# Plain fp32 operands on TensorE for the first batch element of a local attention, with its probabilities transposed there

## The chip, the cores and the metric

The kernel runs on one core of a Trainium2 chip. The metric is the device time of one execution in microseconds, the median of the runs; three runs of the kernel before took 1001.03 to 1006.15 us, with a median of 1003.59.

## What is computed

```python
def _attn_ref(q, k, v, n_global, n_local):          # 4 elements, 8 heads, 768 positions, 64 wide
    scores = scale * np.matmul(q, k.transpose(0, 1, 3, 2))
    keep = is_global | is_local                     # first 8 keys, or the last 96 up to the query
    scores = np.where(keep, scores + bias, -1e9)    # bias: -slope of the head * distance
    a = np.exp(scores - max); a = a / (sum + 1e-9)
    return np.matmul(a, v)
...
x = attn_out as 3072 tokens x 512
h = max(x @ w1, x @ w2, x @ w3, 0); x = h @ w_out   # "MoE 1", no experts, 768 wide
e_idx = argmax(x @ w_gate)                          # "MoE 2": each token goes to one of 8 experts
out[token] = gate * eom * (max(x @ w1[e], 0) @ w2[e])
```

q, k, v are float32; w1, w2, w3 and w_out arrive as float64.

## The kernel before

Attention goes by 24 query tiles of 128 positions, six to a batch element (`QT`), each with 8 heads. A tile sees at most 232 keys: 8 global ones, the 96 before it and its own 128 (the first tile of an element only its own 128).

All products keep fp32's precision by split operands. `a_T` transposes q and k on TensorE, ScalarE writes the high part as fp32r and VectorE the rest (`qh`, `ql`); `a_scores` then does three matmuls per head, high x high, high x low, low x high, in two halves of four heads, after which VectorE adds the bias and takes the minimum (L826) and ScalarE the exponential (L833). `a_trans` splits the probabilities of a half into two fp16 parts (`nat`, L847 and the subtraction at L189) and has the DMA queue transpose them (L853). `a_v` scales v by a power of two and splits it into two fp16 parts; `a_vg` brings the rows of the global keys along and rescales them. `a_out` multiplies with three fp16 matmuls per head and key block (L883), divides on VectorE (L889) and stores the tile; the x of the tiles goes to MoE 1.

MoE 1 takes tiles in passes: eight of two tiles (`m_1`, L976: 216 fp32r matmuls of 256 columns for w1, w2 and w3, 72 each), then two of four tiles with 512 columns. Pass 0 goes through all of w1, then w2, then w3. x is transposed and split first (`split_T`, L917). `m_2` multiplies with w_out (L1036), and `m_route` sends the tokens to their experts. The float64 rows of the weights, 12 for w1 to w3 and 6 for w_out, are loaded as raw words and turned into two fp32r parts by `convert`: ScalarE (L603), VectorE (L605 and twice L608), ScalarE again (L613) and POOL (L189). `pad_rows` stores rows of padding when attention is over. After phase 1 comes a loop over pairs of expert tiles with rows of 25 us per step, bound by TensorE.

The order of all this is written out by `Plan.run`: a list scheduler in the kernel's own Python that takes, again and again, the operation which can start first by its table of costs, ties going to the lower rank. Each engine, and SyncE with the DMA queue, then runs its list strictly in order. A change to one step's costs or waits thus moves others too.

Of the kernel before, what the change touches and what calls it, by code (L numbers as in the profile page):

```python
# [266 lines left out]
def local_attention_moe_kernel(  # L267
# [25 lines left out]
    QT = S // P  # L293
    NTILE = NT // P

    NPAIR = NTILE // 2 - 4
# [187 lines left out]
    for tag, n in (("qk", 4),):  # L484
        stock(tag, [at.tile([P, H, HD], F32, name=f"{tag}n{c}") for c in range(n)])
    stock("va", [at.tile([P, 2, D], F16, name=f"va{c}") for c in range(4)])
    vs = at.tile([P, NTILE, 4], F32, name="vs")
    stock("qT", [[at.tile([P, H // 2, P], F32R, name=n) for n in ("qh", "ql")]])
    stock("kT", [at.tile([P, 2, H // 2, NW], F32R, name=f"k{c}") for c in range(2)])
    stock("sp", [at.tile([P, 4, NW], F32, name=f"sp{c}") for c in range(2)])  # L490


    nat_t = [at.tile([P, 2, 4, 2 * P], F16, name=f"nat{c}") for c in range(2)]
    stock("nat", nat_t)
    stock("aT", [at.tile([P, 2, 4, 2, P], F16, name=f"aT{c}") for c in range(2)])
    stock("xo", [at.tile([P, D], F32, name="xo")])
# [4 lines left out]

    scales = [-(2.0 ** (8.0 * j / H)) / HD**0.5 for j in range(2)]

    def tables(rel, key, mask, tmp):
# [132 lines left out]
    def done(tag, u):  # L637

        n = uses[tag, u] = uses.get((tag, u), 0) + 1
        last = u % QT == QT - 1  # L640

        if n == (3 - last if tag == "k" else 1 + (u % QT < QT - 1) + (u % QT < QT - 2)):
            give(dict(k="kT").get(tag, tag), A[tag, u])

    left0 = [0]

    def first_done():
        left0[0] += 1
        if left0[0] == 3:
# [5 lines left out]
    def a_load(u, name):  # L655
        b, i = divmod(u, QT)
        if u == 0:
            t = Buf(first["qkv".index(name)])
            t.written = t.last = 5.5 + 1.46 * "qkv".index(name)
        else:  # L660
            t = yield take("qk")
        if u or name == "v":
            yield dma(P * D * 4, w=[t], rate=DMA_RATE_ROWS)
            src = [x[b, :, i * P : (i + 1) * P, :].rearrange("h t d -> t h d") for x in (dict(q=q, k=k, v=v)[name], vd)]
            if name == "v":
                nc.sync.dma_start(out=t.t, in_=src[1], cond=dense > 0, cond_hint=False)
                yield op(DMA, 0.5)
                nc.sync.dma_start(out=t.t, in_=src[0], cond=dense < 1, cond_hint=True)
            else:
                nc.sync.dma_start(out=t.t, in_=src[0])  # L670
        return t

    def a_v(u):

        if u:
            yield need(("va", u - 1))
        t = yield from a_load(u, "v")
        va = yield take("va")
        vf = t.t.rearrange("p h d -> p (h d)")
        b, i = divmod(u, QT)  # L680
        sb = VS[u]
        total, top, scale, ratio = [vs[:, u, n : n + 1] for n in range(4)]
        before = vs[:, u - 1, 1:2] if i else VLOW
# [24 lines left out]
        if u:  # L708
            give("qk", t)
        else:  # L710
            first_done()
        A["va", u] = va
        state("va", u)

    def a_vg(u):

        yield need(("va", u), ("o", u - 1))
        va = A["va", u - 1]
        rows = slice(G0, P - NPREV)
        first_ = u % QT == 1  # L720
        src = va if first_ else A["va", u - 2]
        yield dma(0, [src], [va])
        nc.sync.dma_start(out=va.t[rows], in_=src.t[:NG] if first_ else src.t[rows])
        if not first_:
            done("va", u - 2)
        eng = yield op((ACT, POOL), {ACT: act(2 * D), POOL: pool(2 * D)}, [VS[u], va], [va])
        if eng == ACT:
            nc.scalar.mul(out=va.t, in_=va.t, mul=vs[:, u, 3:4])
        else:
            nc.gpsimd.tensor_scalar(out=va.t, in0=va.t, scalar1=vs[:, u, 3:4], scalar2=None, op0=ALU.mult)  # L730
        state("vg", u)

    def a_T(u, name):
# [9 lines left out]
        else:  # L743
            new = yield take("qT")
        A[name, u] = new
        bank = yield take("bank")
# [4 lines left out]
        if u:  # L751
            give("qk", t)
        else:
            first_done()
        if name == "q":
            h, l = new.t[0], new.t[1]
# [13 lines left out]
        if name == "k" and i:  # L770
            old = A["k", u - 1]
            g0 = NB if i == 1 else 0
            yield op(ACT, act(H * NG), [old], [new])
            nc.scalar.copy(out=new.t[:, :, :, :NG], in_=old.t[:, :, :, g0 : g0 + NG].bitcast(F32))
# [5 lines left out]
    def a_scores(u, qd):  # L780
# [25 lines left out]
        for hp in range(2):  # L806
            for j in range(2):
                h = 2 * (2 * qd + hp) + j
                o = sp.t[:, 2 * hp + j, n0:]
                x = sc[j][:, hp, :nw_]  # L810
# [26 lines left out]
    def a_trans(u, qd):  # L837
        i = u % QT
        n0 = NB if i == 0 else 0
        yield need(("s", u, qd), *([("t", u, 0)] if qd else [("t", u - 1, 1)] if u else []))  # L840
        sp = A["sp", u, qd]
        nat = yield take("nat")
        h, l = [nat.t[:, n, :, G0 + n0 :] for n in range(2)]
        x = sp.t[:, :, n0:]
        n = 4 * (NW - n0)
# [4 lines left out]
        give("sp", sp)  # L850
        aT = yield take("aT")
        yield dma(P * 16 * P * 2, [nat], [aT], True, DMA_RATE_ROWS)
        nc.sync.dma_start_transpose(  # L853
# [6 lines left out]
    def a_out(u):  # L860
# [3 lines left out]
        sm = ms.t[1]  # L864
        va, vb = A["va", u], A["va", u - 1] if i else None
        yield op(DVE, 0.37, [ms, VS[u]], [ms])
        nc.vector.tensor_scalar(out=sm, in0=sm, scalar1=1.0e-9, scalar2=vs[:, u, 2:3], op0=ALU.add, op1=ALU.mult)
        nc.vector.reciprocal(out=sm, in_=sm)
        bank = yield take("bank")
        po = bank.t.rearrange("p (h d) -> p h d", d=HD)  # L870
        for h in range(H):
# [3 lines left out]
            for part, vp in ((1, va), (0, vb)):  # L875
                if vp is None:
                    continue
                for n, m_ in ((0, 2), (1, 1)):
# [24 lines left out]
        if vb:  # L903
            done("va", u - 1)

# [761 lines left out]
    with tc.manual_schedule(engines={ET.PE, ET.Activation, ET.DVE, ET.Pool, ET.SP}):  # L1667
# [83 lines left out]
```

## Time and profile before

| | |
|---|---|
| Median of three runs | 1003.59 us |
| The profiled execution | 1000.66 us, of which its span 998.8 |
| TensorE matmuls busy | 929.9 us (93%) |
| TensorE weight loads busy | 798.7 us (80%) |
| VectorE busy | 650.0 us (65%) |
| ScalarE busy | 518.7 us (52%) |
| GpSimd (POOL) busy | 184.9 us (19%) |
| Mean granted TensorE clock | 0.983 |

Busy time of matmuls includes their way through the array, so neighbours overlap: rates are read from the starts of instructions that follow each other. PE is TensorE's matmuls, PEld its weight loads, DVE VectorE, ACT ScalarE, SP the engine that issues the DMAs. A name in brackets behind a row is what ended the idle time before it.

### The profile page before, as it was taken

How to read it: one execution, taken by the hardware profiler on the slowest of the kernel's cores; microseconds unless marked ns; L12 is line 12 of the kernel's file. 1: busy time of each engine (PE TensorE's matmuls, PEld its weight loads, DVE VectorE, ACT ScalarE, POOL GpSimd, SP SyncE). 2: the span in 40 equal slices, each digit the busy share in tenths (PEclk: the TensorE clock that was granted, in tenths of full speed). 3: DMA queues.
4: the chain of work that ended last, by engine and by line, in shares of the span. 5: the costliest groups of instructions: out<-in, count | busy, mean ns of one | idle time of the engine just before them, and what ended most of it. 6: DMA issues, size and time to landing. Idle time of an engine off the chain costs nothing. (4 is left out here: it accounts for less than half of the span.)

```text
span 998.8 us, 19937 instructions
## 1 busy us (share of the span) xinstructions
PE 929.9 (93%) x6640; PEld 798.7 (80%) x6640; DVE 650.0 (65%) x1761; ACT 518.7 (52%) x1111; POOL 184.9 (19%) x242
## 2 busy tenths in 40 slices
PE   2486899999999999999799999999999999999996
PEld 2385788989999999999588787778888888888884
DVE  5989877777777777764433435676666666666664
ACT  4767567666556675752212312435555555555552
POOL 2544324322221321120000101120000000000000
PEclk9997999999999999999799999999999999999998
DMA  7889288667757585643711106166666666666665
GB/s 202 231 218 231 65 148 162 148 137 162 149 121 154 124 175 123 150 97 95 203 43 43 43 22 230 44 232 230 209 201 210 205 210 201 213 210 197 210 219 176
DMA packets 222798, 160.80 MB, mean 161 GB/s; under 512 B 181344, under 2 KB 181344, under 8 KB 222724
## 3 DMA queue, kind: packets, MB, share of 16 engines
q1 hardware_dynamic: 218562, 147.23, 55.5%
q0 software_dynamic: 4160, 12.62, 3.5%
q8 instruction: 41, 0.67, 0.3%
q14 instruction: 33, 0.27, 0.1%
q10 hardware_dynamic: 2, 0.00, 0.0%
HBM read 118.56 MB, written 23.11 MB: 142 GB/s over the span
## 5 line engine op out<-in xcount | busy, mean ns | idle before, releaser
L976 PE MATMUL bank<-xT,w 128*128 128x256 f32 x1728 | 233.5, 290 | 2.0 <-DVE xT L189 1.0
L976 PEld LDWEIGHTS bank<-xT,w 128*128 128x128 f32 x1728 | 217.3, 194 | 7.7 <-ACT xT L920 3.4
L833 ACT ACTIVATE sp<-sp,mn 128x232 f32<-128x232 f32 (+1 forms) x192 | 90.3, 471 | 44.9 <-DVE mn L826 42.9
L976 PE MATMUL bank<-wq,w 128*128 128x512 f32 x432 | 102.9, 397 | 3.3 <-DVE hm L998 2.4
L1458 PE MATMUL bank<-w,hh 128*128 128x512 f32 x426 | 103.3, 394 | 0.0
L976 PEld LDWEIGHTS bank<-wq,w 128*128 128x128 f32 x432 | 81.7, 191 | 21.9 <-DVE hm L998 3.7
L1458 PEld LDWEIGHTS bank<-w,hh 128*128 128x128 f32 x426 | 78.9, 188 | 16.4
L998 DVE TENSOR_TENSOR hm<-hm,bank 128x512 f32<-128x512 f32 x72 | 49.2, 685 | 59.8 <-PE bank L976 58.9
L1537 ACT ACTIVATE hm<-bank 128x512 f32<-128x512 f32 x52 | 31.0, 597 | 93.0 <-PE bank L1531 86.9
L1531 PE MATMUL bank<-wq,xT 128*128 128x512 f32 x312 | 76.5, 394 | 1.2 <-ACTq L1708 1.2
L1036 PE MATMUL bank<-w,hh 128*128 128x512 f32 x288 | 75.8, 404 | 0.0
L1531 PEld LDWEIGHTS bank<-wq,xT 128*128 128x128 f32 x312 | 57.5, 188 | 12.8 <-issue 1.6
L826 DVE CUSTOM_DVE_ANT_0 sp<-bank,bias 128x232 f32<-128x232 f32 x160 | 60.0, 389 | 10.5 <-PE bank L802 10.1
L703 POOL TENSOR_SCALAR qkn<-qkn,vs 128x512 f32<-128x512 f32 x23 | 38.3, 1667 | 142.8 <-DVE vs L698 53.7
L802 PE MATMUL bank<-k,qh 64*128 64x232 f32 (+1 forms) x384 | 43.9, 318 | 20.8 <-ACT k L776 16.4
L1136 POOL DMA_INDIRECT xs<-x2r,di x24 | 24.5, 1022 | 205.9 <-DVE cco L1439 61.9
L189 DVE TENSOR_TENSOR wq<-ws_more,wq 128x1024 fp32r<-128x1024 f32 x42 | 51.3, 1222 | 15.4 <-ACT wq L1382 15.0
L1036 PEld LDWEIGHTS bank<-w,hh 128*128 128x128 f32 x288 | 51.1, 189 | 9.1
L802 PEld LDWEIGHTS bank<-k,qh 64*128 64x128 f32 x384 | 32.2, 205 | 29.9 <-ACT k L776 17.5
L189 DVE TENSOR_TENSOR w<-ws_more,w 128x1024 fp32r<-128x1024 f32 x42 | 51.4, 1225 | 5.8 <-ACT w L1382 5.8
L189 DVE TENSOR_TENSOR nat<-sp,nat 128x928 f16<-128x928 f32 (+1 forms) x46 | 53.3, 1160 | 0.6
L189 POOL TENSOR_TENSOR seen<-x,dco 128x1 f32<-128x1 f32 x14 | 3.4, 245 | 271.2 <-DVE x L1463 271.2
(265 smaller groups left out, 1780.4 us busy)
## 6 DMA issues: line engine op xcount, KB each, us to landing
ws_more<-in_moe_w_dram SPq DMA_DIRECT2D x90, 512.0 KB, 4.4
bias<-in_moe_w_dram SPq DMA_DIRECT2D x19, 512.0 KB, 3.5
ws<-in_moe_w_dram SPq DMA_DIRECT2D x19, 512.0 KB, 4.7
raw<-in_moe_w_dram SPq DMA_DIRECT2D x12, 768.0 KB
x2r<-xs SPq DMA_DIRECT2D x30, 257.0 KB, 3.7
qkn<-in_q_dram SPq DMA_DIRECT2D x23, 256.0 KB
qkn<-in_k_dram SPq DMA_DIRECT2D x23, 256.0 KB
qkn<-vd SPq DMA_DIRECT2D x23, 256.0 KB
```

Source lines behind the costliest of these rows:

```text
L189: eng.tensor_tensor(out=out, in0=in0, in1=in1, op=ALU.subtract)
L703: nc.gpsimd.tensor_scalar(out=vf, in0=vf, scalar1=scale, scalar2=None, op0=ALU.mult)
L802: nc.tensor.matmul(sc[j][:, hp, :nw_], lhsT=x, rhs=y, start=(n < 2), stop=(n >= len(terms) - 2))
L826: nc.vector.tensor_tensor_reduce(out=o[:, g:], in0=x[:, g:], in1=bias[:, pr, n0 + g :], scale=scale, scalar=low, op0=ALU.add, op1=ALU.min, ...
L833: nc.scalar.activation(out=o, in_=o, func=AF.Exp, scale=-1.0, bias=mn[:, h : h + 1], accum_out=sm[:, h : h + 1])
L976: nc.tensor.matmul(pj[:, f2, :], lhsT=w_at(j, part, d)[:, fs], rhs=X[:, d, :], start=(d + n == 0), stop=(d == KD - 1 and n == 2))
L998: nc.vector.tensor_max(out=hv, in0=hv, in1=pj)
L1036: nc.tensor.matmul(bank.t, lhsT=X[:, f, t * P : (t + 1) * P], rhs=w_at(3, part, f), start=(f + n == 0), stop=(f == KF - 1 and n == 2))
L1136: i = nc.gpsimd.indirect_dma_start(out=xs[:, :], out_offset=bass.IndirectOffsetOnAxis(ap=di[:, 0:1], axis=0), in_=x2.t[:, :], in_offset=None)
L1458: nc.tensor.matmul(py, lhsT=at(A_), rhs=w, start=(f + m == 0), stop=(last and m == 2))
L1531: nc.tensor.matmul(ph, lhsT=xT[A_][:, d, :], rhs=W[d][B_][:, b], start=(d + m == 0), stop=(d == KD - 1 and m == 2))
L1537: nc.scalar.activation(out=hm_t[f], in_=ph, func=AF.Relu)
```

## The change

The six tiles of the first batch element (`u < EARLY`) keep q, k and v as plain fp32. Scores are one matmul per head instead of three, the output one per head and key block instead of three. The probabilities stay fp32 and are transposed by TensorE into a PSUM bank, 128 keys at a time, which ScalarE or VectorE copies out. v is loaded straight into its place, with no scaling or parts. The buffers get their old shapes and types back (`renewed`) when the tiles of the second element first take them; the `nat` buffers are cleared by POOL after the first output (`clear_nat`), and `sp` has 24 columns of zeros in front. The rest of the kernel is as it was, but for the order.

```diff
+    EARLY = 6
...
+    def clear_nat():
+        yield need(("o", 0))
+        for t in nat_t:
+            yield op(POOL, 1.2)
+            nc.gpsimd.memset(t[:, :, :, :P], 0.0)
+        state("nat")
...
 def a_v(u, again=False):
+        if u < EARLY and not again:
+            va = yield take("va")
+            yield from a_load(u, "v", va)
+            A["va", u] = va
+            state("va", u)
+            return
...
 def a_T(u, name):
+        if u < EARLY:
+            eng = yield op((ACT, DVE), {ACT: act(D), DVE: dve(D)}, [bank], [new], port=False)
+            if name == "q" and eng == ACT:
+                nc.scalar.mul(out=new.t[0], in_=pt, mul=qs)
...
+            if name == "k" and i:
+                old = A["k", u - 1]
+                g0 = NB if i == 1 else 0
+                for n0, n1, o0 in ((0, NG, g0), (NG, NB, NW - NPREV)):
+                    n = (n1 - n0) * H // 2
+                    eng = yield op((ACT, DVE, POOL), {ACT: act(n), DVE: dve(n // 2), POOL: pool(n)}, [old], [new])
...
 def a_scores(u, qd):
-            terms = [(r, j, q_.t[x][r, pr], k_.t[r, y, pr, n0:]) for x, y in TERMS for j, r in enumerate(rows)]
-            yield op(PE, 0.1 + len(terms) // 2 * 0.109, [q_, k_], [b0, b1])
+            terms = [(r, j, q_.t[x][r, pr], k_.t[r, y, pr, n0:]) for x, y in (TERMS if u >= EARLY else TERMS[:1]) for j, r in enumerate(rows)]
+            yield op(PE, 0.1 + (len(terms) // 2 * 0.109 if u >= EARLY else 4 * 0.109), [q_, k_], [b0, b1])
...
 def a_trans(u, qd):
+        if u < EARLY:
+            aT = yield take("aT")
+            for part in range(i == 0, 2):
+                bank = yield take("bank")
+                pt = bank.t.rearrange("p (a b) -> p a b", b=P)
+                for h in range(4):
+                    yield op(PE, 0.109, [sp], [bank])
+                    nc.tensor.transpose(pt[:, h, :], sp.t[:, h, part * P : (part + 1) * P], ident)
+                eng = yield op((ACT, DVE), {ACT: act(D), DVE: dve(D)}, [bank], [aT], port=False)
+                (nc.scalar.copy if eng == ACT else nc.vector.tensor_copy)(out=aT.t[:, part], in_=pt)
+                give("bank", bank)
+            give("sp", sp)
...
 def a_out(u):
+                if u < EARLY:
+                    terms.append((aT.t[:, part, h % 4, :], vp.t[:, c]))
+                    continue
...
-            yield op(PE, len(terms) * 0.029, [aT, va] + ([vb] if vb else []), [bank])
+            yield op(PE, len(terms) * (0.029 if u >= EARLY else 0.13), [aT, va] + ([vb] if vb else []), [bank])
...
+        if u == EARLY - 1 and EARLY % QT:
+            plan.add(a_v(u, True), (2, u, 1), HOLD_A)
...
-        for t in nat_t:
-            nc.vector.memset(t[:, :, :, :P], 0.0)
+        for t in sp_t:
+            nc.vector.memset(t[:, :, :G0], 0.0)
+        plan.add(clear_nat(), (5, 0))
```

Three places show how the order moves. The first is SyncE's queue in the start (before; `first` and `qkn` hold q, k and v, `raw` the words of weight rows, `aT` the transposed probabilities):

```order
L668 DMA first_87<-in_v_dram 128x8x64
L670 DMA qkn_561<-in_q_dram 128x8x64
L670 DMA qkn_562<-in_k_dram 128x8x64
L589 DMA raw_75<-in_moe_w_dram 128x1536 x2
L853 DMA_TRANSPOSE aT_578<-nat_576 128x16x128
L853 DMA_TRANSPOSE aT_579<-nat_577 128x16x128
```

The same queue with the change (`vf` is the fp32 v):

```order
L712 DMA vf_565<-in_v_dram 128x8x64
L712 DMA vf_566<-in_v_dram 128x8x64
L714 DMA qkn_561<-in_q_dram 128x8x64
L714 DMA qkn_562<-in_k_dram 128x8x64
L712 DMA vf_567<-in_v_dram 128x8x64
L624 DMA raw_75<-in_moe_w_dram 128x1536
L712 DMA vf_568<-in_v_dram 128x8x64
```

The transposes are gone from the queue, and the v loads of tiles 1 to 3 stand ahead of weight rows.

The second is VectorE's queue up to the first tile's output, before (L826 and L819 are the bias and minimum, printed as ISA):

```order
L608 SCALAR_TENSOR_TENSOR x2r<-raw_74,x2r 128x768
L847 CAST nat_577<-sp_575 128x4x128
L189 TENSOR_TENSOR nat_577<-sp_575,nat_577 128x4x128
L189 TENSOR_TENSOR k_573<-bank_520,k_573 128x4x128
L867 TENSOR_SCALAR sm_582<-sm_582,vs 128x8
L868 RECIPROCAL sm_582<-sm_582 128x8
L608 SCALAR_TENSOR_TENSOR x2r<-raw_74,x2r 128x768
```

and with the change:

```order
L643 SCALAR_TENSOR_TENSOR x2r<-raw_74,x2r 128x768
L836 COPY kf_572<-kf_571 128x4x96
L948 COPY aTf_578<-bank_517 128x512
L982 TENSOR_SCALAR sm_581<-sm_581 128x8
L985 RECIPROCAL sm_581<-sm_581 128x8
```

The two fp16 steps and k's low part are gone; a copy of k and one eviction of transposed probabilities stand in their place.

The third is TensorE's queue from the last attention output on, before (`x` is a tile of MoE 1's input, `wq` holds the transposed x of the passes of four tiles):

```order
L883 MATMUL bank_522<-va_568,aT_579 128x64
...
L917 MATMUL bank_523<-ident,x_536 128x128 x4
L917 MATMUL bank_518<-ident,x_537 128x128 x4
...
L917 MATMUL bank_517<-ident,x_536 128x128
...
L917 MATMUL bank_522<-ident,x_537 128x128 x4
...
L976 MATMUL bank_516<-wq,w_740 128x512 x3
```

and with the change:

```order
L1003 MATMUL bank_519<-va_1528,aT_1920 128x64
L1096 MATMUL bank_522<-xT_625,w_705 128x256
...
L1037 MATMUL bank_521<-ident,x_536 128x128 x4
L1037 MATMUL bank_523<-ident,x_537 128x128 x3
...
L1037 MATMUL bank_520<-ident,x_536 128x128 x4
...
L1037 MATMUL bank_519<-ident,x_537 128x128 x4
...
```

Before, only w_out matmuls stand between the last output and the four transposes of x, and no MoE matmul of 256 columns follows. With the change 213 of them follow the last output: 12 ahead of the first x, 57 ahead of the third, 96 ahead of the fourth.

## Rows read from the trace of the kernel before

**Rows 1.** Busy time in three stretches: start:end, length, then columns as named above them
```profile
core 0: us, PE busy (x) PEld busy (x) DVE busy (x) ACT busy (x) POOL busy (x), PEclk, DMA share, GB/s
0.00:57.00 57.00, 22.64 (x180) 18.33 (x180) 43.17 (x130) 35.21 (x81) 23.91 (x46) 1.00 0.82 227
57.00:112.00 55.00, 41.42 (x400) 38.91 (x399) 48.42 (x103) 40.28 (x88) 20.90 (x14) 0.87 0.75 189
...
475.50:488.00 12.50, 6.90 (x32) 4.95 (x33) 5.92 (x30) 2.98 (x12) 0.00 (x0) 0.69 1.02 246
```

**Rows 2.** TensorE's timeline: start us, length us, instruction, [idle before, releaser]
```profile
57.54 5.03 PE L976 MATMUL bank<-xT,w 128*128 128x256 f32 x29 [0.34 <-DVE xT L189]
...
92.48 2.63 PE L976 MATMUL bank<-xT,w 128*128 128x256 f32 x12
...
111.92 9.08 PE L976 MATMUL bank<-xT,w 128*128 128x256 f32 x62 [0.67 <-DVE xT L189]
```

**Rows 3.** TensorE's timeline, for the rates
```profile
71.41 6.02 PE L976 MATMUL bank<-xT,w 128*128 128x256 f32 x48
77.27 1.57 PE L883 MATMUL bank<-va,aT 128*128 128x64 f16 x48
78.68 0.60 PE L976 MATMUL bank<-xT,w 128*128 128x256 f32 x3
...
126.85 0.49 PE L802 MATMUL bank<-k,qh 64*128 64x232 f32 x4
...
127.71 1.09 PE L750 MATMUL bank<-ident,qkn 128*128 128x128 f32 x8
128.56 4.36 PE L1036 MATMUL bank<-w,hh 128*128 128x512 f32 x18
...
141.71 0.39 PE L1079 MATMUL bank<-two,lg 32*128 32x16 f32 x2
142.03 1.68 PE L976 MATMUL bank<-xT,w 128*128 128x256 f32 x12
```

**Rows 4.** Waits of the DMA queue up to 130 us: total us, times, longest
```profile
SPq L853 <- DVE nat L189: 24.3, 5, 15.3
```

**Rows 5.** VectorE's instructions by line and form up to 130 us: busy us, mean ns
```profile
L608 DVE SCALAR_TENSOR_TENSOR wf<-raw,wf 128x768 int32<-128x768 int32 x12 | 12.8, 1070 | 0.2
...
L608 DVE SCALAR_TENSOR_TENSOR x2r<-raw,x2r 128x768 int32<-128x768 int32 x12 | 12.3, 1022 | 0.2
...
L189 DVE TENSOR_TENSOR nat<-sp,nat 128x928 f16<-128x928 f32 x8 | 11.1, 1387 | 0.1
...
L605 DVE TENSOR_SCALAR wf<-wf 128x768 int32<-128x768 int32 x6 | 5.6, 936 | 0.0
...
L605 DVE TENSOR_SCALAR x2r<-x2r 128x768 int32<-128x768 int32 x6 | 3.3, 545 | 0.0
```

**Rows 6.** VectorE's timeline in the start
```profile
10.86 0.68 DVE L189 TENSOR_TENSOR k<-bank,k 128x512 fp32r<-128x512 f32 x1
...
15.15 0.17 DVE L819 CUSTOM_DVE_ANT_0 sp<-bank,bias 128x8 f32<-128x8 f32 x1 [1.69 <-POOL bias L541]
...
15.62 0.40 DVE L515 SCALAR_TENSOR_TENSOR bias<-hm 128x232 f32<-128x232 f32 x1
...
29.42 0.40 DVE L826 CUSTOM_DVE_ANT_0 sp<-bank,bias 128x232 f32<-128x232 f32 x1
...
29.74 0.40 DVE L826 CUSTOM_DVE_ANT_0 sp<-bank,bias 128x232 f32<-128x232 f32 x1
```

**Rows 7.** POOL's timeline: the low parts of the last rows of w3
```profile
88.86 4.54 POOL L189 TENSOR_TENSOR w<-wf,w 128x768 fp32r<-128x768 f32 x2 [5.21 <-ACT w L613]
```

**Rows 8.** TensorE's timeline after the last attention output
```profile
475.57 0.55 PE L917 MATMUL bank<-ident,x2r 128*128 128x128 f32 x3 [0.20 <-ACT x2r L1047]
...
481.31 0.48 PE L917 MATMUL bank<-ident,x 128*128 128x128 f32 x1 [4.61 <-DMA x<-xd]
...
486.51 1.22 PE L976 MATMUL bank<-wq,w 128*128 128x512 f32 x2 [0.78 <-DVE wq L189]
```

More of the change, by code (lines that the diff above doesn't have):

```diff
@@ L485, in local_attention_moe_kernel, with early, renewed, fp16_v @@
         stock(tag, [at.tile([P, H, HD], F32, name=f"{tag}n{c}") for c in range(n)])
[L486 to L490 removed]
+    again = {}
+    def early(tag, tiles):
+        stock(tag, [t for t, _ in tiles])
+        for b, (_, later) in zip(plan.idle[tag], tiles):
+            again[id(b)] = later
+    def renewed(b):
+        later = again.pop(id(b), None)
+        if later:
+            b.t = later()
+    def fp16_v(c):
+        return at.tile([P, D], F32, tag=f"va{c}", name=f"vf{c}"), lambda: at.tile([P, 2, D], F16, tag=f"va{c}", name=f"va{c}")
+    def split_k(c):
+        shape = [P, 2, H // 2, NW]
+        return at.tile(shape, F32, tag=f"k{c}", name=f"kf{c}"), lambda: at.tile(shape, F32R, tag=f"k{c}", name=f"k{c}")
+    def fp16_a(c):
+        return (
+            at.tile([P, 2, 4, P], F32, tag=f"aT{c}", name=f"aTf{c}"),
+            lambda: at.tile([P, 2, 4, 2, P], F16, tag=f"aT{c}", name=f"aT{c}"),
+        )
+    early("va", [fp16_v(c) for c in range(4)])
+    vs = at.tile([P, NTILE, 4], F32, name="vs")
+    q_shape = [P, H // 2, P]
+    early("qT", [([at.tile(q_shape, F32, tag="qh", name="qf")], lambda: [at.tile(q_shape, F32R, tag=n, name=n) for n in ("qh", "ql")])])
+    early("kT", [split_k(c) for c in range(2)])
+    sp_t = [at.tile([P, 4, 2 * P], F32, name=f"sp{c}") for c in range(2)]
+    stock("sp", sp_t)
     nat_t = [at.tile([P, 2, 4, 2 * P], F16, name=f"nat{c}") for c in range(2)]
     stock("nat", nat_t)
[L495 removed]
+    early("aT", [fp16_a(c) for c in range(2)])
     stock("xo", [at.tile([P, D], F32, name="xo")])
@@ L639, in done @@
         n = uses[tag, u] = uses.get((tag, u), 0) + 1
-        last = u % QT == QT - 1
-        if n == (3 - last if tag == "k" else 1 + (u % QT < QT - 1) + (u % QT < QT - 2)):
-            give(dict(k="kT").get(tag, tag), A[tag, u])
+        i = u % QT
+        if tag == "k":
+            left = 3 - (i == QT - 1)
+        elif tag == "vx":
+            left = 1 + (i < QT - 2)
+        else:
+            left = 1 + (i < QT - 1 and u != EARLY - 1) + (i < QT - 2 and u not in (EARLY - 1, EARLY - 2))
+        if n == left:
+            give(dict(k="kT", vx="va").get(tag, tag), A[tag, u])
     left0 = [0]
@@ L653, in first_done, with a_load @@
             give("xT", xb)
-    def a_load(u, name):
+    def a_load(u, name, t=None):
         b, i = divmod(u, QT)
-        if u == 0:
+        flat = t is not None
+        if flat:
+            pass
+        elif u == 0:
             t = Buf(first["qkv".index(name)])
@@ L671, in a_load, with v_of, a_v @@
         return t
-    def a_v(u):
-        if u:
-            yield need(("va", u - 1))
+    def v_of(u, user):
+        return ("vx" if u == EARLY - 1 and user >= EARLY else "va"), u
+    def a_v(u, again=False):
+        if again:
+            yield need(("q", u))
+        elif u:
+            yield need(("va", u - 1), *([("vx", u - 1)] if u == EARLY and u % QT else []))
+        if u < EARLY and not again:
[4 more added lines that the diff above has]
+            return
         t = yield from a_load(u, "v")
+        if again:
+            yield dma(0, w=[t])
+            nc.sync.dma_start(out=t.t[G0 : G0 + NG], in_=v[u // QT, :, 0:NG, :].rearrange("h t d -> t h d"))
         va = yield take("va")
+        renewed(va)
         vf = t.t.rearrange("p h d -> p (h d)")
@@ L707, in a_v @@
         sub(nc.gpsimd, va.t[:, 1, :], vf, va.t[:, 0, :])
[L708 to L713, printed above, removed]
+        give("qk", t)
+        what = "vx" if again else "va"
+        A[what, u] = va
+        state(what, u)
     def a_vg(u):
         yield need(("va", u), ("o", u - 1))
-        va = A["va", u - 1]
+        va = A[v_of(u - 1, u)]
         rows = slice(G0, P - NPREV)
         first_ = u % QT == 1
[L721 to L725, printed above, removed]
+        if u != EARLY:
+            src = va if first_ else A[v_of(u - 2, u)]
+            yield dma(0, [src], [va])
+            nc.sync.dma_start(out=va.t[rows], in_=src.t[:NG] if first_ else src.t[rows])
+            if not first_:
+                done(*v_of(u - 2, u))
+        if u < EARLY:
+            state("vg", u)
+            return
         eng = yield op((ACT, POOL), {ACT: act(2 * D), POOL: pool(2 * D)}, [VS[u], va], [va])
@@ L744, in a_T @@
             new = yield take("qT")
+        if u >= EARLY:
+            renewed(new)
         A[name, u] = new
@@ L754, in a_T @@
             first_done()
+        if u < EARLY:
+            eng = yield op((ACT, DVE), {ACT: act(D), DVE: dve(D)}, [bank], [new], port=False)
+            if name == "q" and eng == ACT:
+                nc.scalar.mul(out=new.t[0], in_=pt, mul=qs)
+            elif name == "q":
+                nc.vector.tensor_scalar(out=new.t[0], in0=pt, scalar1=qs, scalar2=None, op0=ALU.mult)
+            else:
+                (nc.scalar.copy if eng == ACT else nc.vector.tensor_copy)(out=new.t[:, 0, :, off : off + P], in_=pt)
+            give("bank", bank)
[5 more added lines that the diff above has]
+                    eng = yield op((ACT, DVE, POOL), {ACT: act(n), DVE: dve(n // 2), POOL: pool(n)}, [old], [new])
+                    copy = {ACT: nc.scalar.copy, DVE: nc.vector.tensor_copy, POOL: nc.gpsimd.tensor_copy}[eng]
+                    copy(out=new.t[:, 0, :, n0:n1], in_=old.t[:, 0, :, o0 : o0 + n1 - n0])
+                done("k", u - 1)
+            state(name, u)
+            return
         if name == "q":
@@ L772, in a_T @@
             g0 = NB if i == 1 else 0
+            if u == EARLY:
+                for n0, n1, o0 in ((0, NG, g0), (NG, NB, NW - NPREV)):
+                    n = (n1 - n0) * H // 2
+                    h, l = [new.t[:, j, :, n0:n1] for j in range(2)]
+                    x = old.t[:, 0, :, o0 : o0 + n1 - n0]
+                    yield op(ACT, act(n), [old], [new])
+                    nc.scalar.copy(out=h, in_=x)
+                    yield op(DVE, dve(n), [old, new], [new])
+                    sub(nc.vector, l, x, h.bitcast(F32))
+                done("k", u - 1)
+                state(name, u)
+                return
             yield op(ACT, act(H * NG), [old], [new])
@@ L864, in a_out @@
         sm = ms.t[1]
-        va, vb = A["va", u], A["va", u - 1] if i else None
+        va, vb = A["va", u], A[v_of(u - 1, u)] if i else None
         yield op(DVE, 0.37, [ms, VS[u]], [ms])
-        nc.vector.tensor_scalar(out=sm, in0=sm, scalar1=1.0e-9, scalar2=vs[:, u, 2:3], op0=ALU.add, op1=ALU.mult)
+        if u < EARLY:
+            nc.vector.tensor_scalar_add(out=sm, in0=sm, scalar1=1.0e-9)
+        else:
+            nc.vector.tensor_scalar(out=sm, in0=sm, scalar1=1.0e-9, scalar2=vs[:, u, 2:3], op0=ALU.add, op1=ALU.mult)
         nc.vector.reciprocal(out=sm, in_=sm)
@@ L903, in a_out @@
         if vb:
-            done("va", u - 1)
+            done(*v_of(u - 1, u))
     X_AT = {}
```

20 lines of the change are left out of this document (15 added, 5 removed).

## The prediction

> **What bounds the kernel now.** I read the busy time by stretches first, then TensorE's timeline, then VectorE's, then the waits of the DMA queue. The reader is to see three stretches. Up to 57 us TensorE is busy for 22.64 us only and VectorE for 43.17; from 57 to 112 it is 41.42 against 48.42 of 55 [rows 1]. From 111.92 us the timeline shows TensorE without a gap until about 475, so behind that point only TensorE's own work counts. Then a hole comes, with a granted clock of 0.69 [rows 1], and later the expert loop, which the change doesn't touch. So the start and the hole are where time can be won, and added TensorE work costs its full length wherever TensorE is already full.
>
> The landmarks of the start: the first expert-free layer (pass 0, tiles 0 and 1) starts at 57.54, released by tile 1's transposed x; its last third, on w3, starts at 92.48; pass 1 starts at 111.92 [rows 2].
>
> **TensorE's rates.** From consecutive starts [rows 3]: a MoE matmul of 256 columns 5.86/48 = 0.122 us; a 64-column fp16 output matmul 1.41/48 = 0.0294; half a tile's scores (12 matmuls) 0.86; a fp32 transpose 0.85/8 = 0.106.
>
> Up to 111.92 TensorE has done 52 q/k transposes (5.5 us), 10 score halves (8.6), 168 output matmuls (4.9), 16 x transposes (1.7) and 216 MoE matmuls (26.4): 47.1 us. It has lost 64.8 us to idleness and to running slowly.
>
> **What the change adds on TensorE**, for six tiles.
> - 88 transposes of probabilities, priced as the q/k ones: 9.3 us.
> - Output: 88 plain fp32 matmuls for 264 fp16 ones (7.8 us). The only plain fp32 matmul of the trace is the router's [rows 3]: two records per matmul, together 0.39 us long, next start 0.32 after. A record is 0.278 long, so the two start 0.11 apart. I take 0.22, where weight loads follow each other without a change of shape; 0.32 is the upper bound, and two fp16 steps, 0.06, the lower. 19.4 - 7.8 = +11.6 (-2.5 to +20.4).
> - Scores: 4 plain matmuls per half for 12. A plain fp32 column costs up to 0.106/128 = 0.83 ns by the transpose, an fp32r column 0.122/256 = 0.48. With two records of 0.19 us and the two heads going together, a half is 0.77, so -1.1 in all for 12 halves. Lower bound 8 records at today's 0.07: 0.56. Upper bound four streams of 0.11 one after another for each of the 4 matmuls: 1.77. So -3.6 to +10.9. I take 0.77 since today's two heads overlap too: 12 matmuls of 232 columns in 0.86.
>
> Sum +19.8 us (3 to 41). The Trainium skill, page "FP8 and Floating Point Precision", section "TensorE Precision Notes", says "True FP32: 4 passes through PE array". That speaks against the change, since four passes take the place of three products; by it a score half is 0.9 to 1.8 us and the sum 21 to 32. The trace shows two records and not what is inside one.
>
> **What it removes.** VectorE loses both low parts of q and k (0.7 each), the fp16 low part of the probabilities (1.39 for half a tile) [rows 5], some fp16 copies and the chain on v; it gains part of the evictions of transposes, about 0.6 each by rows of the same size. ScalarE takes most of those and loses the two v activations, the scaling of v's global rows and the fp16 copies: cost nothing, it is busy 35 of 57 us [rows 1]. POOL loses two v operations per tile and gains two clears of nat, no more than the 2.3 us each that one of its weight rows takes; it waits for ScalarE anyhow [rows 7]. The DMA queue loses the transposes of these tiles. It spent 24.3 us holding one for VectorE's low part [rows 4], with the loads of weights, q and k behind it. What it gets instead are waits at x stores and global-row copies, which wait for the output; four v loads move ahead of q, k and weights, some 0.8 MB more, about 4 us at 227 GB/s, under VectorE's tables.
>
> **The new start**, counted along VectorE's order.
> - First score: 15.15 now, behind the POOL tables that wait for the flags; k's low part at 10.86 and q's before it leave that queue [rows 6], 1.3 us together, so 13.8.
> - Up to tile 1's x: 8 scores of tile 0 at 0.47 (3.8), 10 at 0.32 (3.2) [rows 6], two bias rows 0.6, six weight rows, each 34.0/12 = 2.8 less the overlap = 2.6 [rows 5] (15.6), two outputs 2.0, two x low parts 1.2, copies 1.2: 27.6. To this I add 5 us in which VectorE stands behind output rows whose matmuls are slower now. Pass 0 starts at 47, not 57.5.
> - Up to w3's last row: six weight rows 15.6, ten scores 3.2, router constants 1.3, five evictions 3.0, one output's divisors 0.4: 23.5, with 2 of waits 72; then 0.8 on ScalarE and up to 4.5 on POOL for its last two rows [rows 7]: 77 against 92.5.
> - Then on TensorE: 72 MoE matmuls 8.8, the rest of tile 3 (a score half, 8 transposes, an output) and two x: 6.0. That is 92; I add 5 for evictions that the in-order queue must wait for (today 13.6 us are idle from 57 to 112). Pass 1 starts at 97.
>
> Up to there TensorE does 44 q/k transposes, 9 score halves, 56 transposes of probabilities, 56 output matmuls, 16 x transposes and 216 MoE matmuls: 4.7 + 6.9 + 5.9 + 12.3 + 1.7 + 26.4 = 57.9. Lost: 39.1. So the start gives 64.8 - 39.1 - 19.8 = **5.9 us**.
>
> **The hole.** Now the last pair pass ends before attention does. The next x tiles are loaded behind seven pad stores: 4.6 us of wait, then a slow clock and 0.8 us for wq, from 475.57 to 486.51 [rows 8]. Inside that is about 2.7 us of work, so 8.2 are lost. In the new order 213 of the last pair pass's 216 matmuls follow the last output, 26 us, and the pads are interleaved with the x loads. I take **6 us**, leaving 2.2 for the third x tile, which has only 57 of them (7 us) as cover for its pads and its load. Nothing else is counted: the loop's steps depend on the experts' counts alone.
>
> Sum: 5.9 + 6 = 11.9; 1000.66 - 11.9 = 988.8 for an execution like the profiled one. The median of the runs, 1003.59, lies 2.9 above it, so 991.7, in round numbers **991**.
>
> **Rivals.**
> - *The start does not get shorter* (0.18): weight rows are held by another thing, the x stores in the DMA queue or VectorE behind outputs. For it: DMA share 0.82 and 0.75 [rows 1]. Against: the transposes' traffic goes too. Pass 1 at 106: 1000.7.
> - *Plain fp32 is dear* (0.14), the one on the other side: four streams per score matmul, one head after another, and 0.32 per output matmul. TensorE gets 19.8 + 12.0 + 8.8 = 41 us instead of 19.8. Part can hide in the start, so 1003 to 1013; since tile 1's output lies on the path to pass 0 I say 1010. It decides from 32 us of added work on (64.8 - 39.1 + 6). For it: the router's next start [rows 3]. Against: two records per matmul, heads that overlap today. The page of the Trainium skill quoted above would have four passes too.
> - *The hole stays* (0.13): x loads still land late or the clock falls there. 997.7.
> - That the change is not made as said I exclude: the order has 96 score matmuls and 176 output rows fewer and 88 transposes more. EARLY equals the tiles of one element, so the second copy of v is never made.
>
> **How the numbers follow.** My forecast has 0.55, with its own range 981 to 997. A measurement can tell 0.5%, 5 us, from no change: faster is below 998.6, slower above 1008.6. Faster: 0.53 + 0.07 (half of the staying hole) + 0.03 = 0.63. Same: 0.02 + 0.13 + 0.06 + 0.04 = 0.25. Slower: 0.10 + 0.02 = 0.12. The range goes up to 1006, leaving out most of the dear fp32, and down to 981.
>
> **What would show it.** Right: first MoE matmul near 47 us, w3's third near 77, pass 1 near 97, no idle of several us behind the last output, plain output matmuls 0.2 to 0.25 apart. Wrong: score halves above 1.5 us, pass 1 after 105, or gaps in TensorE between 110 and 450, which would mean that the new evictions hold it.

## The result, and the profile after

The changed kernel takes **1012.23 us** (median of 6 runs, 1008.97 to 1014.3). The kernel before, run beside it, takes 1003.68. The ratio is 1.0081 [1.0054, 1.0108]: slower by 0.8%. I had forecast 991, with a range from 981 to 1006: the time went up where I had it going down. The profiled execution took 1008.97 us, of which its span 1007.2; its mean granted clock is 0.984, against 0.983 before.

Busy time by stretches (the view of [rows 1]) after the change, with the place of the hole as a third stretch:

```profile
core 0: us, PE busy (x) PEld busy (x) DVE busy (x) ACT busy (x) POOL busy (x), PEclk, DMA share, GB/s
0.00:57.00 57.00, 37.44 (x184) 29.37 (x184) 32.63 (x112) 31.59 (x74) 18.99 (x46) 0.91 0.79 227
57.00:112.00 55.00, 52.61 (x414) 48.46 (x410) 44.87 (x101) 37.46 (x88) 20.08 (x14) 0.97 0.46 127
440.00:475.00 35.00, 24.75 (x194) 23.92 (x194) 11.41 (x44) 6.17 (x16) 4.12 (x15) 0.85 0.48 143
```

In the start TensorE is now busy for 37.44 and 52.61 us instead of 22.64 and 41.42, and VectorE has 10.5 us less in the first stretch. The load went from one engine to the other as meant. The third row shows what I had not expected: in 35 us at the end of attention TensorE is busy for 24.75 only, at a clock of 0.85.

TensorE's timeline of the start, with the landmarks of [rows 2] and the rates:

```profile
48.44 0.38 PE L1096 MATMUL bank<-xT,w 128*128 128x256 f32 x1 [0.31 <-ACT xT L1040]
49.81 5.28 PE L1096 MATMUL bank<-xT,w 128*128 128x256 f32 x23 [0.99 <-DVE xT L189]
...
56.04 0.66 PE L946 MATMUL bank<-ident,sp 128*128 128x128 f32 x4
...
70.04 3.68 PE L1003 MATMUL bank<-vf,aTf 128*128 128x64 f32 x32
73.53 3.12 PE L1096 MATMUL bank<-xT,w 128*128 128x256 f32 x24
76.57 1.05 PE L899 MATMUL bank<-kf,qf 64*128 64x232 f32 x8
77.56 0.66 PE L946 MATMUL bank<-ident,sp 128*128 128x128 f32 x4
...
78.92 0.63 PE L946 MATMUL bank<-ident,sp 128*128 128x128 f32 x4
79.30 3.11 PE L1096 MATMUL bank<-xT,w 128*128 128x256 f32 x24
...
83.33 0.98 PE L1096 MATMUL bank<-xT,w 128*128 128x256 f32 x6
...
105.46 2.76 PE L1096 MATMUL bank<-xT,w 128*128 128x256 f32 x21
```

Pass 0 starts at 48.4 us (its first matmul alone; the others follow from 49.8), w3's third at 83.3, pass 1 at 105.5; I had said 47, 77 and 97. The rates: 32 records of output matmuls in 73.53 - 70.04 = 3.49 us, two records to a matmul, so 0.218 each (forecast 0.22). A score half 77.56 - 76.57 = 0.99 (forecast 0.77, before 0.86). Four transposes of probabilities 79.30 - 78.92 = 0.38, where others start 0.49 apart; some 0.10 each. For six tiles that adds 8.8 for the transposes, 88 x 0.218 - 7.8 = 11.4 for the output and 12 x 0.13 = 1.6 for the scores: **21.8 us**, against 19.8 forecast.

VectorE in the same stretch:

```profile
56.74 0.69 DVE L948 COPY aTf<-bank 128x512 f32<-128x512 f32 x1 [5.88 <-PE bank L946]
```

VectorE stands for 5.88 us before a copy of transposed probabilities, because TensorE takes the MoE matmuls from 48.44 on, and half a tile's scores, first; the transposes start at 56.04. The next two instructions on weight rows start only at 58.11.

TensorE after the last attention output (the place of [rows 8]):

```profile
448.13 3.47 PE L1096 MATMUL bank<-xT,w 128*128 128x256 f32 x27
457.14 1.11 PE L1037 MATMUL bank<-ident,x 128*128 128x128 f32 x4 [5.54 <-DMA x<-xd]
457.90 6.76 PE L1096 MATMUL bank<-xT,w 128*128 128x256 f32 x39
469.37 1.12 PE L1037 MATMUL bank<-ident,x 128*128 128x128 f32 x4 [4.71 <-DMA x<-xd]
470.14 15.25 PE L1096 MATMUL bank<-xT,w 128*128 128x256 f32 x117
```

The hole has become two, 5.54 and 4.71 us, each waiting for a load of x. Behind them the matmuls start slow: 39 take 6.76 us, 0.17 each against 0.12 in [rows 3]. Together some 13.8 us are lost (10.3 of waits, and an estimate of 3.5 for matmuls slower than 0.122), where I had counted 8.2 before and 2.2 after. The DMA queue shows why:

```profile
452.30 0.81 SPq L611 DMA_DIRECT2D xs<-x2r  x2
453.21 0.40 SPq L1058 DMA_DIRECT2D x<-xd  x1
453.66 12.07 SPq L611 DMA_DIRECT2D xs<-x2r  x5
465.83 0.38 SPq L1058 DMA_DIRECT2D x<-xd  x1
```

and the queue's waits from 440 to 475 us (total, times, longest):

```profile
SPq L611 <- DMA xs<-x2r,di: 17.9, 2, 9.4
```

The stores of padding (line 611, `pad_rows`) write the same tensor `xs` as the indirect stores of routed tokens (`xs<-x2r,di`), and they wait for those, 17.9 us in two waits. The loads of x (line 1058) stand behind them in the queue. Now that the pads come while the router still sends tokens, they have something to wait for. In the kernel before they came 19 us later, from 471.39 on, and waited there only for POOL (3.8 us) and for plain stores to `xs` (2.2).

Last, one wait in the middle of attention that the kernel before doesn't have:

```profile
366.31 0.98 PE L1096 MATMUL bank<-xT,w 128*128 128x256 f32 x6
369.39 0.16 PE L750 MATMUL bank<-vs,ones 128*128 128x1 bf16 x1 [2.10 <-ACT va L746]
369.42 3.74 PE L1096 MATMUL bank<-xT,w 128*128 128x256 f32 x18
```

The 2.10 us are followed by 18 matmuls in 3.74 us, where 2.2 would do.

### The profile page after: what moved, and what is told of

It reads as the page before. It is cut to its first block, busy times and chain, and to the rows that moved or that the text cites. A ratio compares the mean times of both kernels' runs of the same rounds, so it can differ in the third digit from the quotient of the medians.

```text
span 1007.2 us, 19730 instructions
## 1 busy us (share of the span) xinstructions
PE 958.1 (95%) x6586; PEld 821.8 (82%) x6586; DVE 622.8 (62%) x1716; ACT 502.4 (50%) x1089; POOL 171.3 (17%) x239
## 4 chain that ended last, share of the span: by engine, by line
PE 86%; DVE 5%; DMA 4%; issue 2%; ACT 1%; POOL 1%; SPq 1%; POOLq 0%; ACTq 0%; DVEq 0%
PE bank L1096 28%; PE bank L1651 14%; PE bank L1578 14%; PE bank L1156 9%; PE bank L1003 5%; PE bank L899 4%; PE bank L1635 3%; PE bank L1037 2%; PE bank L815 2%; PE bank L1543 1%; DVE wf L643 1%; PE bank L1187 1%; DMA ws<-in_moe_w_dram 1%; PE bank L946 1%; PE bank L1603 1%
## 5 line engine op out<-in xcount | busy, mean ns | idle before, releaser
L1096 PE MATMUL bank<-xT,w 128*128 128x256 f32 x1728 | 236.3, 293 | 1.3 <-DVE xT L189 1.0
L1096 PEld LDWEIGHTS bank<-xT,w 128*128 128x128 f32 x1728 | 220.3, 197 | 6.5 <-issue 2.8
L1118 DVE TENSOR_TENSOR hm<-hm,bank 128x512 f32<-128x512 f32 x72 | 49.3, 685 | 70.4 <-PE bank L1096 67.3
L1502 ACT CAST w<-ws_more 128x1024 fp32r<-128x1024 f32 x42 | 44.3, 1055 | 13.9 <-PE bank L1578 10.1
L189 DVE TENSOR_TENSOR wq<-bias,wq 128x1024 fp32r<-128x1024 f32 x14 | 17.2, 1225 | 48.6 <-ACT wq L1502 48.6
L1651 PE MATMUL bank<-w,xT 128*128 128x512 f32 x156 | 46.8, 408 | 0.0
L1502 ACT CAST wq<-ws_more 128x1024 fp32r<-128x1024 f32 x41 | 41.7, 1048 | 9.6 <-PE bank L1578 9.6
```

The source lines that it names most:

```text
L189: eng.tensor_tensor(out=out, in0=in0, in1=in1, op=ALU.subtract)
L1096: nc.tensor.matmul(pj[:, f2, :], lhsT=w_at(j, part, d)[:, fs], rhs=X[:, d, :], start=(d + n == 0), stop=(d == KD - 1 and n == 2))
L1118: nc.vector.tensor_max(out=hv, in0=hv, in1=pj)
L1502: (nc.scalar.copy if eng == ACT else nc.vector.tensor_copy)(out=h, in_=s.t)
L1651: nc.tensor.matmul(ph, lhsT=xT[A_][:, d, :], rhs=W[d][B_][:, b], start=(d + m == 0), stop=(d == KD - 1 and m == 2))
```

## The experiments

Two numbers of each profiled execution split the time well: when pass 1 starts, and when the loop over expert tiles starts. What TensorE has done by pass 1 is the same in all kernels with the same number of early tiles, and the loop and the tail behind it did not change.

| kernel | pass 1 | loop | between | median us | ratio to before, beside it |
|---|---|---|---|---|---|
| before | 111.92 | 665.27 | 553.35 | 1003.68 | |
| changed | 105.46 | 674.11 | 568.65 | 1012.23 | 1.0081 [1.0054, 1.0108] |
| changed, late padding | 106.33 | 660.73 | 554.40 | 995.92 | 0.9929 [0.9905, 0.9953] |
| before, late padding | 113.14 | 660.23 | 547.09 | 993.61 | 0.9898 [0.9873, 0.9924] |
| the same again | 112.95 | 658.32 | 545.37 | 993.64 | 0.9916 [0.9896, 0.9936] |
| rounded scores | 110.43 | 675.02 | 564.59 | 1009.94 | 1.0061 [1.0041, 1.0081] |
| ScalarE copies | 107.55 | 668.13 | 560.58 | 1002.05 | 0.9984 [0.9966, 1.0002] |
| both edits | 103.27 | 653.77 | 550.50 | 989.13 | 0.9881 [0.9854, 0.9908] |
| the same again | 110.17 | 660.63 | 550.46 | 993.48 | 0.9893 [0.9869, 0.9917] |

In the kernel before, the row of [rows 2] that starts at 111.92 begins with the second matmul of pass 1. The first stands alone ahead of it:

```profile
110.86 0.38 PE L976 MATMUL bank<-xT,w 128*128 128x256 f32 x1 [0.68 <-ACT xT L920]
```

The other kernels of the table are read from their first one, so what is taken against the first line is uncertain by 1.1 us. The change thus won 5.4 to 6.5 us up to pass 1 and lost 14.2 to 15.3 behind it. Late padding changes nothing in the order of TensorE and VectorE up to pass 1, so the gain in the start rests on two executions of the changed order (105.46, 106.33) and three of the order before (110.86, 113.14, 112.95).

**Late padding in the changed kernel.** The pads wait until the last x load of the first pass of four tiles is queued.

```diff
             nc.sync.dma_start(out=xb.t, in_=xd[n * P : (n + 1) * P, :])
+            state("xl", seq)
...
-        yield need(("o", NTILE - 1))
+        yield need(("o", NTILE - 1), ("xl", X_SEQ[NPAIR + 1] - 1))
```

> The changed kernel with one edit: the twelve pad stores wait until the x tiles of the first pass of four tiles are loaded, so that no pad store stands ahead of those loads in the DMA queue. Theory (the hole behind attention comes from x loads queued behind pad stores, which wait for the scatter of routed tokens): the two waits of TensorE on x, 5.5 and 4.7 us, and about 3 us of slow clock behind them go; 12 to 14 us faster than the changed kernel, 998 to 1001 us. Rival (the x loads themselves or the slot of x are late): under 3 us faster, 1009 to 1012, with the same waits on x.

Measured 995.92 (994.17 to 998.12), 16.3 below the changed kernel and faster than the kernel before. The queue now has the loads of x first:

```profile
445.85 6.68 SPq L1058 DMA_DIRECT2D x<-xd  x4
456.90 7.61 SPq L611 DMA_DIRECT2D xs<-x2r  x12
```

TensorE has no wait for x left between 440 and 480 us, and the way from pass 1 to the loop is 14.25 us shorter, at the same pass 1 within a microsecond. The hole is shown to cost about that much, and the pads ahead of the x loads are shown to make it. It is more than half of what the forecast missed (the table further down).

**Late padding in the kernel before.** The same edit.

> The kernel before with the same edit. Theory: its hole of 8 us (4.6 of them a wait on x behind pad stores) shrinks to the wait on wq and the x stores; 3 to 8 us faster, 996 to 1001 us. Rival (there the last store of x or the opening of wq is what is late, since no pass of two tiles is left to cover it): under 2 us faster, 1002 to 1004.

Measured 993.61, 9.4 below the kernel before beside it, a larger gain than the 3 to 8 us I had expected; a second time 993.64 (below). From pass 1 to the loop it saves 6.3 and 8.0 us, or 7.3 and 9.0 from the first matmul. So the hole cost 6 to 9 us before and about 14 after: the change made it 5 to 8 us worse instead of 6 better. And with the hole gone from both, the change is still not a gain: 995.92 against 993.61, 2.3 us, which the intervals (0.9905 to 0.9953, 0.9873 to 0.9924) don't fully separate.

**Four early tiles.** `EARLY = 4` in place of 6, padding as in the changed kernel.

> The changed kernel with four plain fp32 tiles instead of six; tiles 4 and 5, whose work lies where TensorE has no gap, get their split operands back (and v of tile 3 a second, split copy). Theory (each plain tile costs TensorE about 3.8 us more: 16 transposes at 0.10, 16 output matmuls at 0.22 for 48 at 0.029, two score halves at 0.99 for 0.86, and from 50 us on that is added to the time in full): 6 to 8 us faster than the changed kernel if the hole stays as it is, 1004 to 1006 us, with the start up to the first MoE matmul as in the changed kernel (near 49 us). Rival (the loss lies in evictions and waits of the start alone): no more than 2 us, 1010 to 1012. The place of the hole moves with the order, so its length is read from the trace apart.

Measured 1006.38 (ratio 1.0040 [1.0024, 1.0057]), 5.8 below the changed kernel. But this run moved the hole as well: TensorE waits there once, for 3.63 us, instead of twice. The edit with late padding, further down, tells the two apart.

**Scores from rounded operands.** q and k of the early tiles are copied out as fp32r, so that a score matmul is one record instead of two.

```diff
-        return at.tile(shape, F32, tag=f"k{c}", name=f"kf{c}"), ...
+        return at.tile(shape, F32R, tag=f"k{c}", name=f"kf{c}"), ...
...
-    early("qT", [([at.tile(q_shape, F32, tag="qh", name="qf")], ...
+    early("qT", [([at.tile(q_shape, F32R, tag="qh", name="qf")], ...
```

> The changed kernel with q and k of the first element rounded to fp32r and one product (their low parts are left out); TensorE's order is row for row the same. Theory (plain fp32 runs as two records per matmul, 0.99 us for a half of the scores, and TensorE is the bound from 50 us on): a half takes 0.3 to 0.4 us, 12 halves save 7 to 8 us of TensorE, of which 5 to 8 show: 1004 to 1007 us. Rival (TensorE waits for evictions, exponentials and weights anyway, and a shorter product only lengthens waits): under 2 us, 1010 to 1012.

Measured 1009.94 (1.0061 [1.0041, 1.0081]), only 2.3 below the changed kernel. A score half went from 0.99 to 0.41 us (77.06 to 77.47), so TensorE had over 5 us less to do up to pass 1, and yet pass 1 started 5 us later, at 110.43. The timeline shows it after tile 3's scores, in this kernel

```profile
89.65 6.92 PE L1003 MATMUL bank<-vf,aTf 128*128 128x64 f32 x32
96.33 6.88 PE L1096 MATMUL bank<-xT,w 128*128 128x256 f32 x45
```

and in the changed kernel

```profile
89.17 4.12 PE L1003 MATMUL bank<-vf,aTf 128*128 128x64 f32 x32
93.09 5.64 PE L1096 MATMUL bank<-xT,w 128*128 128x256 f32 x45
```

The same 32 output records take 6.7 us instead of 3.9. The stretch from 83 to 106 us has a granted clock of 0.70 in the first and 0.93 in the second:

```profile
83.00:106.00 23.00, 20.59 (x121) 19.40 (x119) 15.84 (x36) 12.29 (x30) 6.44 (x5) 0.70 0.25 63
```

```profile
83.00:106.00 23.00, 21.15 (x155) 18.95 (x152) 19.32 (x44) 15.87 (x40) 8.89 (x6) 0.93 0.24 57
```

TensorE stood longer before transposes that wait for exponentials (14.0 us in all up to pass 1, against 9.3), and then got less clock. This is one execution of each kernel, and further down two executions of one kernel differ by more than these 5 us. What the runs show is the median: of the 5 to 8 us that the theory had, 2.3 came. The length of a score half was not the main thing that set the end; that shorter scores make the start later is not shown.

**ScalarE makes the copies.** Every copy of transposed probabilities goes to ScalarE, so that VectorE never stands before one. First with late padding:

```diff
-                eng = yield op((ACT, DVE), {ACT: act(D), DVE: dve(D)}, [bank], [aT], port=False)
+                eng = yield op((ACT,), {ACT: act(D)}, [bank], [aT], port=False)
```

> The changed kernel with late padding (995.9 us), and in addition every copy of transposed probabilities out of PSUM is given to ScalarE, none to VectorE. In the changed kernel VectorE stands from 50.86 to 56.74 us before such a copy, since the transposes are queued on TensorE behind MoE matmuls, and 6 to 8 instructions on weight rows of w2 stand behind it. Theory (the start lost its gain because VectorE, which prepares the weight rows, is made to wait for TensorE): the 5.9 us of wait go, w3's third starts at 77 to 80 us and pass 1 at 99 to 102, time 990 to 993. Rival (TensorE's own added work and ScalarE's exponentials hold the start, VectorE's wait is slack): pass 1 still at 104 to 106, time 994.5 to 998.

Measured 989.13 (987.23 to 994.31), what the theory had and a little more. But the profile doesn't bear out its reason. VectorE's wait of 5.88 is gone and waits at other places are there, the two longest being

```profile
27.81 0.69 DVE L1009 TENSOR_TENSOR x<-bank,sm 128x512 f32<-128x512 f32 x1 [4.61 <-PE bank L1003]
...
60.77 0.40 DVE L923 CUSTOM_DVE_ANT_0 sp<-bank,bias 128x232 f32<-128x232 f32 x1 [2.84 <-PE bank L899]
```

the first of them 3.23 in the changed kernel. The copies now stand between the exponentials on ScalarE. TensorE's transposes wait for those, up to pass 1, in this kernel

```profile
PE bank L946 <- ACT sp L930: 14.9, 9, 6.0
```

and in the changed kernel

```profile
PE bank L946 <- ACT sp L930: 9.3, 8, 5.0
```

Pass 0 starts 3.4 us later than with late padding alone (52.7, 49.3), and pass 1 follows after 50.6 us instead of 57.0. The two other executions with these copies (below) have pass 0 at 55.4 and 57.1, and pass 1 52.2 and 53.1 us behind it. What is won for good lies elsewhere: pass 1 to loop is 550.50 and 550.46 in the two runs, against 554.40 with late padding alone. This 3.9 us is the wait at line 750 with its slow matmuls, which the edit happens to remove: with the edit TensorE is without a gap and at full clock from 360 to 380 us, where late padding alone has 17.86 us busy at 0.91. Here is late padding alone, then with the copies:

```profile
360.00:380.00 20.00, 17.86 (x178) 16.92 (x177) 12.26 (x36) 11.89 (x32) 5.08 (x4) 0.91 0.66 134
```

```profile
360.00:380.00 20.00, 20.00 (x193) 17.84 (x192) 17.00 (x50) 12.75 (x34) 4.65 (x4) 1.00 0.77 169
```

The gap, 2.1 us, and the clock, 0.09 of 17.86, make 3.7. Late padding alone is one execution, and the two of the kernel before with late padding differ by 1.7 us in this number. The other 3 us, the earlier pass 1, didn't come in the second run.

**ScalarE copies without late padding**, and beside it the kernel before with late padding and the changed kernel with both edits once more.

> The changed kernel with one edit: ScalarE makes every copy of transposed probabilities, VectorE none; padding as in the changed kernel. Theory (two separate losses, VectorE's wait in the start and the hole behind the last output): the 6.8 us that this edit gave with late padding come here too, 1003 to 1008, and the hole stays, with waits for x loads behind pads and a slow clock. Rival (the hole takes back what the start gives, since an earlier end of attention brings the pads earlier too): 1009 to 1013.

Measured 1002.05 (0.9984 [0.9966, 1.0002]), 10.2 below the changed kernel. In the profile pass 1 is at 107.55, later than the 105.46 of the changed kernel. Three executions of this start have it at 103.27, 107.55 and 110.17, two of the changed kernel's at 105.46 and 106.33, so no gain in the start is shown; the way to the loop is 8.1 us shorter: 3.9 for the wait at line 750, and a smaller hole, 6.6 us of waits for x in place of 10.3. The rival fell, and the theory's reason with it.

> The kernel before with late padding once more, beside the changed one with both edits on one chip: 992 to 996, as the 993.6 of the first run.

Measured 993.64, as before.

> The changed kernel with late padding and ScalarE's copies once more. Theory (the change is worth its start gain once VectorE and the DMA queue are freed of the two waits): 987 to 991, 3 to 6 below the kernel before with late padding. Rival (the change is worth nothing beside its added work on TensorE; the two kernels are alike): within 2 us of it.

Measured 993.48 (989.26 to 995.88): the rival's answer. In the two sets of runs the changed kernel with both edits stands at 0.9881 and 0.9893, the kernel before with late padding at 0.9898 and 0.9916. It beats the kernel before by 1.1 to 1.2%; whether it beats late padding alone by 2 us can't be told from these runs.

**Fewer early tiles, with late padding.**

> Four tiles instead of six have plain fp32 operands, with late padding. Theory (tiles 4 and 5 give nothing to pass 0, whose start and w3 rows hang on tiles 0 to 3, while their share of TensorE's added work, a third of 21.8 us, is paid wherever TensorE is full): 990 to 994, 2 to 6 below the 995.9 of six tiles with late padding. Rival (each tile gives about what it costs): 995 to 997.

> Three tiles with plain fp32 operands, late padding. Theory: as with four, less 3.6 us of added work, but tile 3's transposes through the DMA queue come back under w2 and w3: 988 to 993. Rival (each tile gives about what it costs): 994.5 to 996.5.

> Two tiles with plain fp32 operands, late padding. Theory: only tiles 0 and 1 lie on the path to the first MoE matmul, so most of the gain of the start (first MoE matmul near 48 instead of 57 us) stays with a third of the added work: 986 to 992, below both 995.9 (six tiles) and 993.6 (none). Rival (each tile gives about what it costs, the start is bound elsewhere): 993.5 to 995.5.

Measured 995.99 (0.9937 [0.9912, 0.9962]), 1000.85 (0.9986 [0.9973, 1.0]) and 1002.84 (1.0003 [0.9991, 1.0016]) for four, three and two tiles. Four tiles are as good as six, so the 5.8 us above are the hole's; three and two are worse, and my theory, that tiles 2 and 3 cost more than they give, fell. Both lose it in the start: pass 1 begins at 121.7 us with two tiles and at 120.6 with three, later even than in the kernel before. What the theory left out is the DMA queue. With two early tiles, the probabilities of tiles 2 and 3 go through it again, and outputs wait for them during pass 0:

```profile
97.88 1.46 PE L1003 MATMUL bank<-va,aT 128*128 128x64 f16 x24 [7.70 <-DMA aT<-nat]
```

TensorE stands 7.70 us for the transposes of half a tile, and the granted clock from 83 to 106 us is 0.63. With three it is tile 3's output that waits, ahead of pass 1:

```profile
115.14 1.46 PE L1003 MATMUL bank<-va,aT 128*128 128x64 f16 x24 [5.87 <-DMA aT<-nat]
```

So tiles 2 and 3 seem to earn their added work by staying off that queue; no run tries the queue apart from the rest of the order, and TensorE also waits for weight rows there (6.4 us with three tiles).

## Why the prediction was wrong

By the accounts of the prediction, in microseconds:

| step | forecast | measured |
|---|---|---|
| added work on TensorE, six tiles | +19.8 | +21.8 |
| lost in the start before pass 1 (64.8 before) | 39.1 | 43.4 |
| the start, from these | -5.9 | +0.4 |
| the hole (8.2 lost before) | -6 | +5.6 |
| a new wait at line 750, with the clock after it | 0 | +3.9 |
| sum | -11.9 | +9.9 |

43.4 is 105.46 less the work done by then, at the measured rates: 52 q/k transposes 5.5, 10 score halves 9.9, 64 transposes of probabilities 6.4, 56 output matmuls 12.2, x 1.7, 216 MoE matmuls 26.4. The profiled executions differ by 1008.97 - 1000.66 = 8.3, so the accounts leave 1.6 us over; the 1.1 us between pass 1's first two matmuls in the kernel before is of that size.

- **The hole failed most**, by 11.6 us. The prediction said that the pads "are interleaved with the x loads" and that 213 matmuls would cover them. It priced the pads as transfers and not as instructions that can wait. Moving attention's end ahead of the routing of the last tokens put them where they wait for the indirect stores, 17.9 us, with the x loads behind. The trace of before shows no pad that waits for an indirect store, but the reason was in the code: two kinds of store to one tensor in one order. Late padding shows it: -16.3 us.
- **The rival "the hole stays"** (0.13) had the right place, with 997.7 too little: the hole grew.
- **The first score, pass 0 and the price of output matmuls were right**: 13.7 (forecast 13.8), 48.4 (47), 0.218 (0.22).
- **From pass 0 to w3's third** I gave 23.5 us of VectorE's own work, 2 of waits and 5.3 behind them; it took 34.9 instead of 30, with the 5.88 us before one copy inside it. For that stretch I had counted what the copies cost VectorE and only 2 us of waits, not whom VectorE waits for there: TensorE, in order, behind MoE matmuls. The ScalarE experiment adds that this wait isn't the whole bound: taken away, it comes back as waits for exponentials, and pass 1 lies between 103 and 110.
- **Pass 1** came 22.1 us after w3's third, forecast 20. The order did eight q/k transposes, eight of probabilities and half a tile's scores more before it than I had counted, some 2.7 us of work.
- **The scores** were mis-sized: 0.99, not 0.77, for a half. The sentence of the Trainium skill that the prediction quoted, page "FP8 and Floating Point Precision", section "TensorE Precision Notes" (four passes for true fp32), gave an estimate of 0.9 to 1.8 for a half and 21 to 32 for the sum; 0.99 and 21.8 agree with its lower ends, and the trace was right that the two heads overlap.
- **From 111.92 us "without a gap until about 475"** held for the kernel before, and I took it to hold after. The new order put one late activation on v ahead of TensorE, 2.10 us, and 3.9 with the clock. Why that activation is late was not tried.

With the price of plain fp32 almost as forecast, the change took 14 us off VectorE up to 112 us (10.5 and 3.6 in the two stretches) and put 21.8 on TensorE, in a start in which neither is the bound alone: pass 1 came 5.4 to 6.5 us earlier, and the added work that lies behind pass 1, 21.8 less the 62.1 - 47.1 = 15.0 done ahead of it, so 6.8 us, took that back. What bounds the start beyond the waits named stays open.

## What to carry to other kernels

A step that becomes early pulls forward everything that is keyed to its end: look in the code, not only in the trace, for what those instructions must wait for at the new time, and what stands behind them in the same queue. When an eviction is moved to another engine, ask first where in its order the producer now runs it; an engine that runs its list in order stops there behind whatever TensorE has to do first, 5.88 us in this kernel. And judge a change with unrelated holes closed on both sides: the edit of two lines that put the pads behind the x loads was worth 0.8 to 1.0% in the kernel before, while the change, once they are so in both kernels, shows no gain (995.92 against 993.61).

## What the runs showed that I had not expected

- **A short idle cost TensorE more than its length.** The 2.10 us at line 750 cost 3.7 to 3.9, and the 10.3 us of the hole 13.8. The granted clock is lower in the stretch with the wait, 0.91 in the mean of the 20 us around the first (with late padding alone): a mean over its two levels, 2.4 and 1.2 GHz.
- **Less work did not give an earlier start of pass 1.** With shorter scores TensorE had over 5 us less to do, and the one execution profiled reached pass 1 5 us later, at a clock of 0.70 instead of 0.93 between 83 and 106 us. How much of this belongs to the kernel and how much to the execution is open, by the next point.
- **The same kernel has two starts.** The two profiled executions of the kernel with both edits run the same order, and pass 1 lies 6.9 us apart, as do their loops; behind pass 1 they agree within 0.04 us. Both have a clock of 0.90 up to 50 us. Here are the two, the one with pass 1 at 103.27 first, from 50 to 83 us, and then TensorE's output of tile 1 and the first MoE matmuls:

```profile
50.00:83.00 33.00, 31.20 (x253) 28.39 (x253) 22.50 (x55) 23.21 (x55) 12.48 (x9) 1.00 0.67 208
```

```profile
50.00:83.00 33.00, 31.39 (x213) 29.20 (x214) 17.96 (x47) 20.59 (x49) 11.51 (x7) 0.79 0.59 185
```

```profile
46.05 4.54 PE L1003 MATMUL bank<-vf,aTf 128*128 128x64 f32 x32
...
53.43 5.54 PE L1097 MATMUL bank<-xT,w 128*128 128x256 f32 x44 [0.34 <-DVE xT L189]
```

```profile
47.55 6.93 PE L1003 MATMUL bank<-vf,aTf 128*128 128x64 f32 x32
...
57.05 8.81 PE L1097 MATMUL bank<-xT,w 128*128 128x256 f32 x45 [0.68 <-ACT xT L1040]
```

The output goes slow in the second (6.93 against 4.54), and the MoE matmuls behind it too (8.81 for 45, against 5.54 for 44). The times of the twelve runs show the same two groups, 987 to 990 us with a mean granted clock of 0.990 to 0.992, and 993 to 996 with 0.985 or 0.986. So in this start a difference of 5 us between two kernels, read from one profile of each, shows nothing by itself; that is also why what the start is bound by stays open beyond the waits named above.
